# A fused attention and feed-forward kernel: the block with both heads' keys on 128 rows from pair 2 on

## The chip, the cores and the metric

The kernel runs on one core of a Trainium2 chip. The metric is the device time of one execution in microseconds. Three runs of the kernel before took 1225.55, 1228.04 and 1230.18 us; their median is 1228.04. The engines are TensorE (PE; its weight loads are shown apart as PEld), VectorE (DVE), ScalarE (ACT), GpSimd (POOL) and SyncE (SP), which issues the transfers.

## The reference

Attention for 4 batches of 12 heads over 448 positions of 64 values, and then two feed-forward layers over the 1792 rows of 768 values that it gives. All inputs and the output are float32.

```python
q_n, k_n = rmsnorm(q, g_q), rmsnorm(k, g_k)
scores = (q_n @ k_n.T) / 8                      # per batch and head, 448 x 448
attn = exp(scores - scores.max(-1)); attn = attn / (attn.sum(-1) + 1e-9)
x = heads_side_by_side(attn @ v)                # 1792 x 768
x = ((x @ w1) * (x @ w2) @ w3) @ w_out          # widths 1024, 1024, 768
h = x @ w_in                                    # width 2048
out = (h * clip(h + 3, 0, 6) / 6) @ w_out2
```

## The kernel before

**Pairs and slots.** The heads are taken in 24 pairs (`NP`), and a pair is worked through in 8 slots, one for each of two heads `j` and four blocks of 112 queries. In a slot `score` (L552) makes the scores of one block in PSUM with two matmuls (L561, L562), DVE scales them and takes their maximum (L568, L575), and ACT takes the exponential with its sum (L580). The values are then in `PP`, with queries on the rows and 2 x 448 keys, both heads side by side, on the columns.

**Blocks of keys.** The product with V needs the keys on the rows, so eight slots later `trans` (L583) turns 128 columns of `PP` at a time with four transposes (L587). The 2 x 448 = 896 columns make seven blocks, `kb` 0 to 6. Blocks 0 to 2 hold keys of the first head and 4 to 6 keys of the second. Block 3 holds both: the last 64 keys of the first head on rows 0 to 63, and 64 keys of the second on rows 64 to 127. The keys of the second head are laid out so that this comes out even.

**High and low parts.** Except in pairs 0 and 1 (`FULL`), a block is multiplied in two parts: `thi` (L593) has ACT write the high part `hi` (L596), rounded to the type fp32r, and `tlo` (L601) has DVE write the rest `lo` (L606). `vo` holds V in the same two parts side by side, 128 columns for each block, and `pv` (L611) adds the products of both parts into a bank of the head (L639 for `hi`, L640 for `lo`).

**Block 3.** For pairs 2 to 11 (`i < K3`, `K3 = 12`) block 3 is made like the others, and `pv` multiplies it with four matmuls of 64 rows each (L627): for each head `j` its own 64 rows of `hi`, and then of `lo`. From pair 12 on the parts are laid out by head: of the first head `hi` takes the high part on rows 0 to 63 (L598) and its low part on rows 64 to 127 (L608); of the second `lo` takes the high part on rows 64 to 127 (L599) and its low part on rows 0 to 63 (L609). Then one matmul of 128 rows for each head (L630) does for high and low together. The V rows of block 3 hold the same 64 keys of a head twice.

**What lies beside it.** TensorE also does the matmuls of the first feed-forward layers between those of the attention: `fill` (L384) emits some of them in every slot, by a budget (`rate`, L786), in threes (L81 to L83), first with weights that are prepared on the way (`wprime`) and then for whole batches (`layer1`, `layer2`). Their weights arrive by DMA as `raw` and are split by ACT (L137, L138, L203, L287), DVE (L140, L143) and POOL (L205, L289). The last layers follow the attention from some 630 us on.

**Order and banks.** The order on each engine comes out of a planner that simulates the program with assumed costs, `schedule_with_timeline_sim` (L982); `issue_after` pins some operations behind others. PSUM has two banks each for scores (`s`), transposes (`t`), attention products (`v`) and feed-forward products (`f`), so a transpose waits until both parts of the block before the last were written.

Of the kernel before, what the change touches and what calls it, by code (L numbers as in the profile page):

```python
# [23 lines left out]
B, H, S, D = 4, 12, 448, 64  # L24
# [15 lines left out]
FULL = (0, 1)  # L40
LG = 8
AHEAD = 3
K3 = 12
SHIFT = {'ssum': -1, 'vsplit': -2, 'load_v': 2, 'rsum1': -1, 'ksplit': 4, 'rms1': 0}


# [1 line left out]
def fused_kernel(ctx: ExitStack, tc: tile.TileContext, nat, qT, kT, vin, gq, gk,  # L48
                 w12, w3t, wo, win, wo2, outT):
    nc = tc.nc  # L50
# [34 lines left out]
    def bank(tag, name="bank"):  # L85
        return pp.tile([P, 512], F32, tag=tag, name=name)
# [317 lines left out]
    T = {}  # L404
    anchors = {}

    def attention(ap, rate):
        def full(i):
            return i in FULL
# [182 lines left out]

        def thi(i, kb):  # L593
            ps, hi, lo = T["X", i, kb]
            if kb != 3 or i < K3 or full(i):
                nc.scalar.activation(hi, ps, AF.Copy)  # L596
            else:
                nc.scalar.activation(hi[0:64, :], ps[0:64, :], AF.Copy)  # L598
                nc.scalar.activation(lo[64:128, :], ps[64:128, :], AF.Copy)  # L599

        def tlo(i, kb):  # L601
            ps, hi, lo = T["X", i, kb]
            if full(i):
                return
            if kb != 3 or i < K3:
                nc.vector.tensor_sub(lo, ps, hi)  # L606
            else:
                nc.vector.tensor_sub(hi[64:128, :], ps[0:64, :], hi[0:64, :])  # L608
                nc.vector.tensor_sub(lo[0:64, :], ps[64:128, :], lo[64:128, :])  # L609

        def pv(i, kb):  # L611
            _, hi, lo = T.pop(("X", i, kb))
            vo = T["V", i]
            if kb == 0:
                T["pv", i, 0] = bank("v")
            if kb == 3:
                T["pv", i, 1] = bank("v")
                for j in range(2):
                    if full(i):
                        z = slice(64 * j, 64 * j + 64)  # L620
                        nc.tensor.matmul(T["pv", i, j][:64, :S], vo[z, j, 3], hi[z, :], start=j == 1, stop=j == 0)
                        continue
                    if i < K3:
                        z = slice(64 * j, 64 * j + 64)
                        w = vo[z, j, 3].rearrange("p a d -> p (a d)")
                        for y in (hi, lo):
                            nc.tensor.matmul(T["pv", i, j][:, :S], w, y[z, :],  # L627
                                             start=(j == 1 and y is hi), stop=(j == 0 and y is lo))
                        continue
                    nc.tensor.matmul(T["pv", i, j][:, :S], vo[:, j, 3].rearrange("p a d -> p (a d)"),  # L630
                                     (hi, lo)[j], start=(j == 1), stop=(j == 0))
                return
            j = kb // 4
            if full(i):
                nc.tensor.matmul(T["pv", i, j][:64, :S], vo[:, j, kb % 4], hi, start=kb == 0, stop=kb == 6)
                return
            w = vo[:, j, kb % 4].rearrange("p a d -> p (a d)")
            ps = T["pv", i, j][:, :S]
            nc.tensor.matmul(ps, w, hi, start=(kb == 0), stop=False)  # L639
            nc.tensor.matmul(ps, w, lo, start=False, stop=(kb == 6))  # L640
# [116 lines left out]
        while t < 8 * NP + 23 or xs_ready:  # L757
            t += 1
            if t == 4:
                first.close()  # L760
            now[0] = t
            live = t < 8 * NP
            ps = score(*divmod(t, 8)) if live else None
            if 0 < t <= 8 * NP:
                expo(*divmod(t - 1, 8))
            u = t - LG
            if 0 <= u < 8 * NP and u % 8 < 7:
                trans(*divmod(u, 8))
            if 0 <= u - 1 < 8 * NP and (u - 1) % 8 < 7:
                tlo(*divmod(u - 1, 8))  # L770
            if live:
                scale_max(t // 8, t % 8, ps)
                negate(*divmod(t, 8))
            if 0 <= u < 8 * NP and u % 8 < 7:
                thi(*divmod(u, 8))
            if 0 <= u - 2 < 8 * NP and (u - 2) % 8 < 7:
                pv(*divmod(u - 2, 8))
            with ExitStack() as es:
                for a in anchors.get(t - (3 if "pool" in L else 2), ()):
                    es.enter_context(tc.issue_after(a.ins))  # L780
                fill(*rate(t))
            run_tasks()
            if "pool" in L:
                xnext()
# [103 lines left out]
    for b, t in enumerate(order):  # L888
        acc = None
        for m in range(M2):  # L890
# [14 lines left out]
            w = wnext  # L905
# [80 lines left out]
```

## Time and profile before

| | |
|---|---|
| median of three runs | 1228.04 us (1225.55 to 1230.18) |
| profiled execution | 1225.79 us, its span 1224.0 us |
| TensorE busy | 1162.5 us (95%) |
| weight loads | 1023.3 us (84%) |
| DVE, ACT, POOL busy | 754.0, 727.5 and 465.5 us |
| read from and written to memory | 173.93 and 28.68 MB |

The span runs from the first to the last instruction of the profiled execution; the time of that execution also counts what lies around it. Busy times overlap between engines. A matmul's duration counts its way through the array, so that successive matmuls overlap; the distance of their starts is what one of them takes of TensorE's time.

### The profile page before, as it was taken

How to read it: one execution, taken by the hardware profiler on the slowest of the kernel's cores; microseconds unless marked ns; L12 is line 12 of the kernel's file. 1: busy time of each engine (PE TensorE's matmuls, PEld its weight loads, DVE VectorE, ACT ScalarE, POOL GpSimd, SP SyncE). 2: the span in 40 equal slices, each digit the busy share in tenths (PEclk: the TensorE clock that was granted, in tenths of full speed). 3: DMA queues.
4: the chain of work that ended last, by engine and by line, in shares of the span. 5: the costliest groups of instructions: out<-in, count | busy, mean ns of one | idle time of the engine just before them, and what ended most of it. 6: DMA issues, size and time to landing. Idle time of an engine off the chain costs nothing.

```text
span 1224.0 us, 16942 instructions
## 1 busy us (share of the span) xinstructions
PE 1162.5 (95%) x5868; PEld 1023.3 (84%) x5868; DVE 754.0 (62%) x1474; ACT 727.5 (59%) x1401; POOL 465.5 (38%) x316
## 2 busy tenths in 40 slices
PE   3698998999899999999999999999999999999998
PEld 2457887777789999889999998999999999999997
DVE  7977988989757787667624446884433433343332
ACT  6888788888767767766534336664433443344332
POOL 3534234544432213221020005555444554554452
PEclk9698998999999999999999999999999999999999
DMA  8677656788887677666359895430200020001001
GB/s 273 213 218 238 187 188 203 249 287 284 281 296 253 209 243 236 231 213 211 137 194 407 323 328 199 155 100 23 91 1 1 1 91 1 1 1 46 1 1 46
DMA packets 64694, 203.73 MB, mean 166 GB/s; under 512 B 8544, under 2 KB 25440, under 8 KB 64608
## 3 DMA queue, kind: packets, MB, share of 16 engines
q1 hardware_dynamic: 64608, 202.65, 49.4%
q8 instruction: 46, 0.75, 0.2%
q14 instruction: 40, 0.33, 0.1%
HBM read 173.93 MB, written 28.68 MB: 166 GB/s over the span
## 4 chain that ended last, share of the span: by engine, by line
PE 68%; ACT 3%; DMA 2%; DVE 1%; issue 1%; POOL 1%; SPq 0%; POOLq 0%; ACTq 0%; DVEq 0%
PE bank L81 7%; PE bank L83 7%; PE bank L82 7%; PE acc L83 6%; PE acc L82 6%; PE acc L81 6%; PE h L81 6%; PE h L82 6%; PE h L83 6%; PE bank L587 2%; PE bank L561 1%; PE bank L562 1%; PE bank L639 1%; PE bank L640 1%; DMA rsb<-rsd 1%; ACT PP L580 1%
## 5 line engine op out<-in xcount | busy, mean ns | idle before, releaser
L847 POOL TENSOR_TENSOR wis<-wf,wis 128x768 fp32r<-128x768 f32 x63 | 120.4, 1911 | 228.1 <-ACT wis L846 228.1
L926 DVE SCALAR_TENSOR_TENSOR u<-u,h 128x448 f32<-128x448 f32 x64 | 39.6, 619 | 210.6 <-ACT u L925 210.6
L847 POOL TENSOR_TENSOR wos<-wf,wos 128x768 fp32r<-128x768 f32 x64 | 120.5, 1883 | 90.4 <-ACT wos L846 89.1
L580 ACT ACTIVATE PP<-PP,mx 112x448 f32<-112x448 f32 x192 | 127.7, 667 | 39.4 <-DVE mx L575 35.0
L568 DVE CUSTOM_DVE_ANT_0 PP<-bank,rb,rq 112x448 f32<-112x448 f32 x192 | 129.2, 676 | 30.7 <-PE bank L562 24.0
L83 PE MATMUL bank<-xhl,ws 128*128 128x448 f32 x384 | 142.1, 370 | 4.6 <-POOL ws L289 4.6
L81 PE MATMUL bank<-xhl,ws 128*128 128x448 f32 x384 | 143.8, 374 | 0.8 <-ACT ws L287 0.8
L82 PE MATMUL bank<-xhl,ws 128*128 128x448 f32 x384 | 141.6, 369 | 0.0
L82 PE MATMUL acc<-g,wos 128*128 128x448 f32 x384 | 141.3, 368 | 0.0
L83 PE MATMUL acc<-g,wos 128*128 128x448 f32 x384 | 141.3, 368 | 0.0
L81 PE MATMUL acc<-g,wos 128*128 128x448 f32 x384 | 139.3, 368 | 0.0
L81 PE MATMUL h<-x2h,wis 128*128 128x448 f32 x378 | 139.0, 368 | 0.0
L83 PE MATMUL h<-x2h,wis 128*128 128x448 f32 x378 | 137.5, 364 | 1.6 <-POOL wis L847 1.6
L82 PE MATMUL h<-x2h,wis 128*128 128x448 f32 x378 | 138.9, 367 | 0.0
L925 ACT ACTIVATE u<-h,half 128x448 f32<-128x448 f32 x64 | 40.8, 637 | 158.0 <-PE h L83 158.0
L930 DVE TENSOR_TENSOR g<-u,g 128x448 fp32r<-128x448 f32 x64 | 103.9, 1623 | 37.4 <-ACT g L929 37.4
L606 DVE TENSOR_TENSOR xl<-bank,xh 128x448 fp32r<-128x448 f32 x142 | 87.3, 617 | 30.7 <-ACT xh L596 29.2
L846 ACT ACTIVATE wos<-wf 128x768 fp32r<-128x768 f32 x64 | 54.2, 847 | 86.0 <-PE acc L83 85.7
L596 ACT ACTIVATE xh<-bank 128x448 fp32r<-128x448 f32 (+1 forms) x156 | 83.3, 541 | 33.0 <-PE bank L587 31.7
L587 PEld LDWEIGHTS bank<-ident,PP 112*128 112x128 f32 x672 | 78.6, 142 | 26.4 <-issue 8.6
L587 PE MATMUL bank<-ident,PP 112*128 112x112 f32 x672 | 95.1, 264 | 5.5 <-DVE xl L606 4.7
L561 PE MATMUL bank<-K,Q 128*112 128x448 f32 x192 | 77.4, 404 | 23.8 <-DVE mx L568 12.7
(136 smaller groups left out, 2754.1 us busy)
## 6 DMA issues: line engine op xcount, KB each, us to landing
ws<-w12d SPq DMA_DIRECT2D x48, 768.0 KB
ws<-wpd SPq DMA_DIRECT2D x32, 768.0 KB
raw<-in_w_dram SPq DMA_DIRECT2D x32, 384.0 KB
w12d<-ws SPq DMA_DIRECT2D x16, 768.0 KB
wr<-in_wo_dram SPq DMA_DIRECT2D x16, 768.0 KB
qr<-in_qT_dram SPq DMA_DIRECT2D x24, 448.0 KB
kr<-in_kT_dram SPq DMA_DIRECT2D x24, 448.0 KB
nat<-in_nat_dram SPq DMA_DIRECT2D x23, 448.0 KB
```

The source lines that it names most:

```text
L81: nc.tensor.matmul(ps, lh, rh, start=first, stop=False)
L82: nc.tensor.matmul(ps, lh, rl, start=False, stop=False)
L83: return nc.tensor.matmul(ps, ll, rh, start=False, stop=last)
L561: nc.tensor.matmul(ps[:CP, :S], qs, k1[:, j, :], start=True, stop=False)
L568: anchors[8 * i + s].append(nc.vector.tensor_tensor_reduce(out=T["PP", i][:, c, sl], in0=ps[:CP, :S], in1=T["rb", i][:, sl], op0=ALU.mult, ...
L580: anchors[8 * i + s].append(nc.scalar.activation(v, v, AF.Exp, bias=T["m", i][:, 8 + s : 9 + s], accum_out=T["sum", i][:, s : s + 1]))
L587: nc.tensor.transpose(ps[:, c * CP : c * CP + CP], src[:, c, kb * P : kb * P + P], ident[:CP, :CP])
L596: nc.scalar.activation(hi, ps, AF.Copy)
L606: nc.vector.tensor_sub(lo, ps, hi)
L846: nc.scalar.activation(t[:, 0, :], wf[q], AF.Copy)
L847: nc.gpsimd.tensor_sub(t[:, 1, :], wf[q], t[:, 0, :])
L930: nc.vector.tensor_sub(g[:, 1, :], u, g[:, 0, :])]
```

## The change

The constant `K3` goes. In `thi`, `tlo` and `pv` the layout by head for block 3 holds for all pairs but 0 and 1, that is from pair 2 on. The four matmuls of 64 rows are removed from the code.

```diff
-K3 = 12
 ...
         def thi(i, kb):
             ps, hi, lo = T["X", i, kb]
-            if kb != 3 or i < K3 or full(i):
+            if kb != 3 or full(i):
                 nc.scalar.activation(hi, ps, AF.Copy)
             else:
                 nc.scalar.activation(hi[0:64, :], ps[0:64, :], AF.Copy)
 ...
-            if kb != 3 or i < K3:
+            if kb != 3:
                 nc.vector.tensor_sub(lo, ps, hi)
             else:
                 nc.vector.tensor_sub(hi[64:128, :], ps[0:64, :], hi[0:64, :])
 ...
-                    if i < K3:
-                        z = slice(64 * j, 64 * j + 64)
-                        w = vo[z, j, 3].rearrange("p a d -> p (a d)")
-                        for y in (hi, lo):
-                            nc.tensor.matmul(T["pv", i, j][:, :S], w, y[z, :],
-                                             start=(j == 1 and y is hi), stop=(j == 0 and y is lo))
-                        continue
                     nc.tensor.matmul(T["pv", i, j][:, :S], vo[:, j, 3].rearrange("p a d -> p (a d)"),
                                      (hi, lo)[j], start=(j == 1), stop=(j == 0))
```

## Rows read from the trace of the kernel before

**Rows 1.** The page: busy us of each engine, share of the span, instructions.
```profile
PE 1162.5 (95%) x5868; PEld 1023.3 (84%) x5868; DVE 754.0 (62%) x1474; ACT 727.5 (59%) x1401; POOL 465.5 (38%) x316
```

**Rows 2.** Windows: stretch, its us, busy us by engine (instructions), clock, DMA, GB/s.
```profile
112.00:142.00 30.00, 30.00 (x175) 27.18 (x175) 21.09 (x48) 19.15 (x42) 12.08 (x10) 1.00 0.74 235
142.00:322.00 180.00, 160.34 (x825) 132.27 (x824) 160.40 (x396) 152.27 (x341) 83.75 (x69) 0.95 0.72 235
322.00:352.00 30.00, 30.00 (x159) 25.46 (x158) 22.71 (x58) 21.22 (x47) 12.68 (x11) 1.00 0.94 321
352.00:640.00 288.00, 286.11 (x1587) 258.79 (x1586) 198.81 (x519) 186.46 (x401) 64.27 (x55) 1.00 0.66 216
```

**Rows 3.** Chain of waits, 324 to 352 us: shares by engine, tile and line.
```profile
by line: PE bank L81 20.5%; PE bank L83 19.7%; PE bank L82 18.8%; PE bank L587 12.1%; PE bank L627 7.1%; PE bank L561 6.4%; PE bank L562 5.8%; PE bank L639 5.1%; PE bank L640 4.6%; PE bank L495 0.4%
```

**Rows 4.** TensorE's waits, 142 to 322 us: us in total, times, longest.
```profile
PE bank L83 <- POOL ws L289: 4.6, 4, 2.7
PE bank L561 <- DVE mx L568: 3.2, 8, 0.5
PE bank L587 <- DVE xl L606: 3.0, 4, 1.4
```

**Rows 5.** By line: ns least/median/most, first and last start; who waited for L599.
```profile
L599 ACT ACTIVATE xl<-bank x12: 539/540/543, 368.9 to 618.5; 64x448 fp32r<-64x448 f32 x12
  DVE xh L608: 6.2, 8
...
L606 DVE TENSOR_TENSOR xl<-bank,xh x142: 570/618/627, 100.9 to 626.3; 128x448 fp32r<-128x448 f32 x142
...
L609 DVE TENSOR_TENSOR xl<-bank,xl x12: 625/626/627, 370.1 to 619.8; 64x448 fp32r<-64x448 f32 x12
```

**Rows 6.** Timeline of TensorE, a block of pair 4: start us, us, instruction.
```profile
161.95 0.34 PE L82 MATMUL bank<-woh,w 128*128 128x384 f32 x1
162.13 0.34 PE L83 MATMUL bank<-woh,w 128*128 128x384 f32 x1
162.40 0.47 PE L627 MATMUL bank<-xh,vo 64*128 64x448 f32 x2
162.80 0.60 PE L587 MATMUL bank<-ident,PP 112*128 112x112 f32 x4
163.33 0.47 PE L627 MATMUL bank<-xl,vo 64*128 64x448 f32 x2
163.73 0.44 PE L81 MATMUL bank<-woh,w 128*128 128x384 f32 x1
164.01 0.34 PE L82 MATMUL bank<-woh,w 128*128 128x384 f32 x1
```

**Rows 7.** Windows of L627 alone: stretch, TensorE busy, weight loads, clock, DMA, GB/s.
```profile
112.00:142.00 30.00, 1.88 (x6) 0.74 (x6) 1.00 0.74 235
142.00:322.00 180.00, 6.68 (x26) 2.65 (x26) 0.95 0.72 235
322.00:352.00 30.00, 2.34 (x8) 0.92 (x8) 1.00 0.94 321
```

**Rows 8.** Timeline of TensorE, a block of pair 12.
```profile
372.88 0.37 PE L630 MATMUL bank<-xh,vo 128*128 128x448 f32 x1
373.09 0.37 PE L81 MATMUL bank<-abh,ws 128*128 128x448 f32 x1
...
373.50 0.55 PE L587 MATMUL bank<-ident,PP 112*128 112x112 f32 x4
373.82 0.45 PE L630 MATMUL bank<-xl,vo 128*128 128x448 f32 x1
374.11 0.55 PE L587 MATMUL bank<-ident,PP 112*128 112x112 f32 x4
```

**Rows 9.** A wait of TensorE (timeline), and the window behind it.
```profile
185.19 0.44 PE L83 MATMUL bank<-woh,w 128*128 128x384 f32 x1 [2.02 <-POOL w L205]
...
185.50:188.90 3.40, 3.40 (x15) 2.42 (x13) 1.77 (x5) 3.40 (x10) 3.22 (x3) 0.54 0.72 221
```

## Prediction

> **What bounds the kernel now.** I read the page first. TensorE is busy for 95% of the span, DVE for 62% and ACT for 59% [rows 1]. So TensorE work taken out is worth its time wherever TensorE never rests, and what is added to DVE and ACT costs time where it makes TensorE rest. The change touches pairs 2 to 11, whose last-block products lie between 119 and 347 us, so I asked for that stretch cut into windows [rows 2]. From 112 to 142 and from 322 to 352 TensorE is busy for every microsecond, with DVE at 70% and 76% and ACT at 64% and 71%. From 142 to 322 TensorE rests for 180 - 160.34 = 19.7 us, DVE is busy for 160.40 (89%) and ACT for 152.27 (85%): three engines that take turns as the one that is late, and the granted clock is 0.95 and not 1.00. From 352 to 640 us TensorE is busy for 286.11 of 288. The chain of waits confirms the second edge: in 324 to 352 us it is TensorE alone, and L627 is 7.1% of it, 2.0 us [rows 3]. The three largest of TensorE's waits in the middle stretch are for POOL's weight halves, 4.6 us, and twice for DVE, 3.2 + 3.0 = 6.2 us [rows 4].
>
> **What TensorE loses: the 64-row visits.** One pair's last block has four matmuls on 64 rows (L627) and gets two on 128 rows (L630). Their durations alone, 4 x 0.47 against 0.37 + 0.45 [rows 6, 8], would give 1.06 us a pair, but matmuls overlap, so I go by starts. In the timeline the two L627 matmuls of a visit stand as one piece, "x2", of 0.47 us: they run side by side on the two halves of the rows [rows 6]. So the four cost two visits, not four turns. A visit still costs more than a turn of a full matmul. From 162.13 to 164.01 are 1.88 us, in which lie L83, two visits with four transposes (L587) between them, and L81. Ordinary starts there are 0.18 apart (161.95 to 162.13); less twice that, the two visits with the transposes take 1.52. In the layout by head, 372.88 to 374.11 are 1.23 us, less 0.41 for the two other matmuls inside (373.09 to 373.50): 0.82 for two L630 and four transposes [rows 8]. One L630 is 0.21 (372.88 to 373.09), so the transposes are 0.40, and a visit is (1.52 - 0.40) / 2 = 0.56. Of it 0.40 pass from its start to the next one; the rest is at its edges, 0.27 us from the L83 before it and 0.28 from the L81 behind it to the next, where 0.18 is usual [rows 6].
>
> The windows for L627 give the visits [rows 7]: 6 matmuls in 1.88 us busy are 4 visits of 0.47 in the first full stretch (one pair's high parts came apart into two), 8 in 2.34 are 5 in the second (the same), and 26 in the middle are 13. 22 visits by 0.56 are 12.3 us. What comes instead is 20 full matmuls by 0.21, 4.2 us. By stretch: first -(4 x 0.56 - 3 x 0.21) = -1.6; second -(5 x 0.56 - 4 x 0.21) = -2.0; middle -(13 x 0.56 - 13 x 0.21) = -4.5. TensorE sheds 8.1 us in all. The bounds are -10.6 (1.06 a pair by bare durations) and -0.4 (a visit at the 0.21 of a turn, so that only the two that came apart are saved).
>
> A rule of the Trainium skill speaks against this change: "TensorE: Matmul & The Clock Gate", Part 3 (Packing small matmuls), The mechanism, has matmuls in different row groups run together in about the time of one, some 4 ns apart, so that four on half the rows would cost what two on all of them cost. This trace agrees that two run as one piece of 0.47 us; it does not agree that the visit is as cheap as a turn, since 0.40 us pass to the next start and not 0.18 to 0.21 [rows 6]. "TensorEngine Tiling (Array Packing)", Tiling Modes, Key Properties, says that changing the mode drains the engine, which would account for the edges.
>
> **What ACT and DVE get.** An operation on 64 rows takes as long as one on 128: L609 on 64 takes 0.626 us, L606 on 128 takes 0.618 [rows 5]. So two for one adds a whole one: 0.54 us of ACT a pair, by L599, and 0.63 of DVE, by L609. From pair 12 on DVE also sat idle for L599 before L608, 6.2 us in 8 of 12 pairs [rows 5], 0.5 us a pair. Neither addition touches a DMA, SP's or POOL's queue. In the full stretches there are 7 and 9 us of DVE left in 30, and 11 and 9 of ACT; 3.5 pairs add some 2.2 and 1.9 us, so they are covered, as pairs 12 to 23 are, where TensorE rested for 1.9 us in 288 [rows 2]. If that cover were gone it would cost 3.5 x 0.63 = 2.2 us.
>
> In the middle 6.5 pairs add 4.1 us to DVE and 3.5 to ACT, in front of operations on which TensorE already waits. Behind L608 and L609 are queued DVE's next score maximum (L568), which frees the score bank, and the next block's L606, which frees the transpose bank; TensorE waits for exactly these [rows 4]. Bounds: at best nothing shows, since ACT and DVE have 28 and 20 us of rest in these 180; at worst each pair's serial chain is longer by 0.54 + 0.63 + 0.5 = 1.67, +10.9 us. I take DVE's 4.1 in full and nothing of ACT's: DVE is as busy as TensorE there, and its two waits together are more than POOL's. The middle then gives -4.5 + 4.1 = -0.4.
>
> **Sum.** -1.6 - 2.0 - 0.4 = -4.0 us. The profiled execution took 1225.79 us (span 1224.0 and 1.8 around it); it would become 1221.8. It lies 2.25 below the median of the runs shown, so against the median it is 1228.04 - 4.0 = 1224.0.
>
> **Rivals.** *All of it arrives.* If DVE's and ACT's operations fit into their 20 and 28 us of rest, the whole 8.1 counts: 1228.0 - 8.1 = 1219.9. For it: TensorE bounds what follows and pairs 12 to 23 run this way without loss. Against: the middle stretch, where TensorE's waits on DVE of 6.2 us show that DVE's rest is not where TensorE needs it.
>
> *The middle is a loop through ACT and DVE: slower.* Transposes, high part, low part, product, with two banks for the transposes. Where this loop and not TensorE sets the pace, the TensorE time saved becomes waiting, and the loop grows by 0.54 + 0.63 in each of 6.5 pairs: +7.6 us. Waits also cost clock: after TensorE had rested 2.02 us before 185.19, the granted clock of 185.5 to 188.9 was 0.54, nearly the lower of its two levels (1.2 of 2.4 GHz) [rows 9]; 3.4 us at 0.54 lose 1.6. Two more such dips are 3.2. With -3.6 from the full stretches: 7.6 + 3.2 - 3.6 = +7.2, 1235. It decides from the point where half of the 6.5 blocks are waited for by TensorE. For it: DVE at 89% and ACT at 85% leave TensorE little that they can do late. Against: the longest wait there, 2.7 us, is for POOL, which gets nothing more to do.
>
> *The visits were free.* If two matmuls side by side take one turn of 0.21 and the time around them belongs to something else, TensorE sheds only 0.4, and DVE's 4.1 in the middle remain: 1228.0 + 3.7 = 1231.7. For it: the two do run as one piece. Against: the starts of rows 6. The first page named above gives this rule in the Trainium skill.
>
> *Another order.* The order on every engine is a planner's, made from assumed costs. Ten pairs of changed operations change the plan from 119 us on, and a wait such as the 2.02 us with the dip of 1.6 behind it [rows 9] may come or go: some 4 us to either side of my sum, 1220 or 1228. Nothing in the trace gives it a sign.
>
> **How the numbers follow.** Chances: my sum 0.38 (its own range 1221 to 1227), all of it 0.24, the slower loop 0.22, free visits 0.07, another order 0.09. About 0.5%, 6.1 us, is what a measurement of this kernel can tell from no change, so faster means under 1221.9 and slower over 1234.2. Faster: 0.20 of the second, 0.06 of my own and 0.03 of the order make 0.29. Slower: 0.16 of the loop and 0.03 of the two others make 0.19. The rest, 0.52, is no change. The range is 1216 to 1236: below, all savings with a wait of 4 us gone besides; above, the loop with its dips and 1 us more.
>
> **What would show it.** Right: no L627; L630 20 times more, with its neighbours 0.21 apart; L598, L599, L608 and L609 22 times each; TensorE still at 100% on either side of the middle; waits on L606, L608 and L609 up by about 4 us in the middle; the stretch after 352 us as long as before. Wrong: waits on DVE and ACT unchanged (then 1220), waits up by over 10 us with more half-clock stretches (1235), or a shift that stands behind POOL or a DMA, which would be the order and not these operations.

## The result, and the profile after

The change made the kernel slower: 1233.57 us against 1226.45, medians of 20 runs each; the ratio is 1.0056 with a 95% interval of 1.0044 to 1.0068, so 6.9 us with 5.4 to 8.3. The forecast of 1224 had the wrong sign, 4.0 us less than a median of three runs that lay 1.6 us above that of the 20; the time lies in the range, near its slow end. The profiled execution of the kernel after took 1229.62 us, 3.8 more than the one of before, so it shows only part of the loss. In the kernel after, the lines of the attention stand one lower, the matmul on 128 rows is L622, the products of the other blocks are L631 and L632.

What the change says, it did. By source line (columns as in [rows 5]) the products on 128 rows are there 22 times for each head, 10 more than the 12 of [rows 5], and so is DVE's first low part (L607), which the first product reads:

```profile
L622 PE MATMUL bank<-xh,vo x22: 363/368/475, 119.1 to 626.8; 128*128 128x448 f32 x22
L622 PE MATMUL bank<-xl,vo x22: 444/450/722, 119.6 to 628.2; 128*128 128x448 f32 x22
...
L607 DVE TENSOR_TENSOR xh<-bank,xh x22: 617/618/619, 113.4 to 622.9; 64x448 fp32r<-64x448 f32 x22
```

The windows answer to [rows 2]:

```profile
112.00:142.00 30.00, 29.30 (x175) 27.35 (x173) 22.87 (x52) 21.01 (x45) 14.07 (x11) 1.00 0.74 231
142.00:322.00 180.00, 155.48 (x791) 129.82 (x792) 167.52 (x395) 150.91 (x333) 78.62 (x67) 0.94 0.71 227
322.00:352.00 30.00, 27.72 (x143) 22.35 (x143) 23.89 (x62) 26.01 (x60) 13.21 (x13) 1.00 0.97 335
352.00:640.00 288.00, 287.47 (x1593) 259.39 (x1592) 199.31 (x525) 188.18 (x405) 65.86 (x55) 1.00 0.67 219
```

TensorE's rest in the middle grew from 19.7 to 24.5 us, and the two stretches in which it never rested have rests of 0.7 and 2.3. DVE is busier in the middle by 7.1 us and TensorE gets 34 matmuls fewer done there (791 for 825). From 352 to 640 us TensorE is as busy as before (287.5 and 286.1 of 288). TensorE's waits from 142 to 322 us answer to [rows 4]:

```profile
PE bank L622 <- DVE xh L607: 8.2, 4, 3.0
PE bank L560 <- DVE mx L567: 4.8, 5, 1.3
PE bank L80 <- ACT ws L286: 3.2, 2, 2.1
PE bank L631 <- ACT xh L595: 2.8, 3, 2.0
PE bank L586 <- DVE xl L605: 2.2, 3, 1.2
PE bank L586 <- DVE xl L608: 1.1, 4, 0.3
...
PE bank L82 <- POOL ws L288: 0.3, 1, 0.3
```

The waits on POOL's weight halves, the largest before, are nearly gone, and a new one leads: the first product on 128 rows waits for DVE, 8.2 us in four places. Before, the high products needed ACT's high part alone; now the first product needs DVE too. The longest of the four, in the timeline of the kernel after (pair 5; lines left out between):

```profile
187.62 0.52 ACT L597 ACTIVATE xh<-bank 64x448 fp32r<-64x448 f32 x1
...
188.10 1.08 DVE L476 TENSOR_TENSOR rt<-ry 112x32 f32<-112x32 f32 x1
188.15 0.54 ACT L598 ACTIVATE xl<-bank 64x448 fp32r<-64x448 f32 x1
...
189.22 0.94 DVE L478 TENSOR_TENSOR rt<-rt,ss 112x32 f32<-112x32 f32 x1
...
190.74 0.90 DVE L483 TENSOR_TENSOR rr<-ry,rt 112x32 f32<-112x32 f32 x1
...
191.67 0.62 DVE L607 TENSOR_TENSOR xh<-bank,xh 64x448 fp32r<-64x448 f32 x1
...
192.32 0.63 DVE L608 TENSOR_TENSOR xl<-bank,xl 64x448 fp32r<-64x448 f32 x1
...
192.34 0.47 PE L622 MATMUL bank<-xh,vo 128*128 128x448 f32 x1 [2.98 <-DVE xh L607]
```

ACT was done at 188.69. DVE came to the block 3 us later, behind other work of its queue. The windows of the kernel after before and behind this wait (columns as in [rows 2]):

```profile
188.80:192.20 3.40, 0.56 (x4) 0.24 (x2) 3.30 (x6) 3.38 (x9) 2.33 (x3) 1.00 0.93 265
194.10:197.50 3.40, 3.01 (x11) 2.45 (x10) 3.19 (x9) 0.69 (x2) 0.00 (x0) 0.51 0.50 202
```

TensorE was busy for 0.56 of 3.4 us, and then the granted clock was 0.51, the lower level, as in [rows 9].

All this could be the cause, or an effect of another order: on TensorE the planner's order differs in many places from 119 us on.

### The profile page after: what moved, and what is told of

Same layout as the page of the kernel before. It is cut to its first block, busy times and chain, and to the rows that moved or that the text cites. A ratio compares the mean times of both kernels' runs of the same rounds, so it can differ in the third digit from the quotient of the medians.

```text
span 1227.8 us, 16926 instructions
## 1 busy us (share of the span) xinstructions
PE 1159.6 (94%) x5848; PEld 1022.4 (83%) x5848; DVE 764.7 (62%) x1484; ACT 734.5 (60%) x1411; POOL 464.2 (38%) x316
## 4 chain that ended last, share of the span: by engine, by line
PE 75%; DMA 7%; ACT 6%; issue 5%; DVE 4%; POOL 3%; SPq 0%; POOLq 0%; ACTq 0%; DVEq 0%
PE bank L80 9%; PE bank L81 9%; PE bank L82 8%; PE acc L80 6%; PE acc L81 6%; PE acc L82 6%; PE h L80 6%; PE h L81 6%; PE h L82 6%; PE bank L586 4%; DMA raw<-in_w_dram 2%; PE bank L560 2%; PE bank L561 2%; PE bank L631 2%; PE bank L632 2%
## 5 line engine op out<-in xcount | busy, mean ns | idle before, releaser
L918 DVE SCALAR_TENSOR_TENSOR u<-u,h 128x448 f32<-128x448 f32 x64 | 39.7, 620 | 210.5 <-ACT u L917 210.5
L80 PE MATMUL h<-x2h,wis 128*128 128x448 f32 x378 | 139.0, 368 | 0.0
L605 DVE TENSOR_TENSOR xl<-bank,xh 128x448 fp32r<-128x448 f32 x132 | 81.2, 616 | 27.2 <-ACT xh L595 25.6
L595 ACT ACTIVATE xh<-bank 128x448 fp32r<-128x448 f32 (+1 forms) x146 | 77.7, 539 | 27.0 <-PE bank L586 24.8
```

The costliest lines, as they stand in the source:

```text
L80: nc.tensor.matmul(ps, lh, rh, start=first, stop=False)
```

## The experiments

Each was timed in five rounds beside the kernel before on the same chip; 1% is 12.3 us. In what follows the loss of 6.9 us is taken apart.

**First round: the planner free.** *low_first* changes only the order of the four products on 64 rows.

```diff
-                        for y in (hi, lo):
+                        for y in (lo, hi):
...
-                                             start=(j == 1 and y is hi), stop=(j == 0 and y is lo))
+                                             start=(j == 1 and y is lo), stop=(j == 0 and y is hi))
```

> The kernel before, with the four 64-row products of block 3 in pairs 2 to 11 in another order: low parts first, then high parts. No work is added; TensorE's first visit then needs DVE's low part, not ACT's high part alone. Theory of the product's wait (the layout by head makes TensorE wait for DVE's queue, 8.2 us at four places in the trace after): slower than before by 5 us or more, 1232 or above, with waits of the first visit on DVE. Theory of DVE's time (0.63 us a pair more on DVE): no change, 1225 to 1228. Theory of the plan (another order of the engines, whatever the edit): anything within 4 us, no such waits.

0.9961 (0.9946 to 0.9977): 4.8 us faster. The forecast of the product's wait missed, but the wait itself was not tested: the trace has no wait of L627 on DVE. The same work in another order moved the time by most of what was to be explained. So an edit with a free planner can't be read as the cost of its operations.

*pe_only* gives TensorE its two products and leaves ACT and DVE as they were (in `pv` alone `if i < K3` becomes `if False`).

> ACT and DVE work as in the kernel before, one operation each for block 3, and TensorE takes the two 128-row products in pairs 2 to 11 all the same: of the high part for the first head, of the low part for the second, so the block's product leaves out half of its terms and mixes heads. TensorE's saving alone. The product's wait: the first product needs ACT alone, so the 8.1 us worked out for TensorE arrive, 1217 to 1221. DVE's time: the same, 1217 to 1221. The plan: 1222 to 1231, no gain that can be told from the order.

1.0007 (0.9986 to 1.0027). TensorE's saving did not arrive, or the order hid it.

*ops_only* adds the work of ACT and DVE alone.

```diff
+            if kb == 3 and i < K3 and not full(i):
+                for z in (slice(0, 64), slice(64, 128)):
+                    nc.scalar.activation(hi[z, :], ps[z, :], AF.Copy)
...
+            if kb == 3 and i < K3:
+                for z in (slice(0, 64), slice(64, 128)):
+                    nc.vector.tensor_sub(lo[z, :], ps[z, :], hi[z, :])
```

> The kernel before, with block 3 in pairs 2 to 11 written by two ACT and two DVE operations of 64 rows each, every half in its own place, and the four 64-row products as before. Only the added work. The product's wait: high products still need ACT alone, so little: 0 to 3 us more, 1226 to 1229.5. DVE's time: 4 to 7 us more, 1230.5 to 1233.5. The plan: anything within 4 us.

1.0046 (1.0029 to 1.0063), 5.6 us: about the loss, without any product on 128 rows.

*late* emits the products of block 3 of the kernel after at the start of the next slot.

> The kernel after, with the two products of block 3 in pairs 2 to 11 emitted at the start of the next slot, behind that slot's feed-forward matmuls, so that DVE has about 2 us more until TensorE comes to them. The product's wait: the waits of L630 on L608 fall from 8.2 to under 2.5 us and most of the loss goes, 1220 to 1227. DVE's time: no change from after, 1232 to 1235. The plan: anything within 4 us of after.

1.0045 (1.0027 to 1.0063), no help. But the test missed its aim: in the trace the first product stands behind the same six feed-forward matmuls as in the kernel after, and the waits of L630 on L608 were still 7.4 us. It tells nothing of the wait.

**Second round: the order held.** The planner's order of the kernel before, instruction by instruction and for every engine, was written into the program as edges from each instruction to the one before it on its engine. An added operation stands right behind the one it was split from, the first product of 128 rows in the place of the high visit, the second in that of the low visit. In the traces TensorE, ACT, DVE and POOL then work through the instructions of before in the same order, so that kernels differ by their operations alone. In the edit, `at` holds one engine's instructions in the order of before.

```diff
+        for y, z in zip(at, at[1:]):
+            tc.add_manual_dep(z[2], y[2].name, mybir.DependencyInfo(mybir.DependencyClass.NoSync, mybir.DependencyReason.DATA), reason='hold')
```

> The kernel before, unchanged, with the order of the instructions of every engine written into it as edges (the order that the planner had found for it). A control: all theories expect the time of before, within 2 us.

1.0001 (0.9984 to 1.0018): holding the order costs nothing that can be told (-2.0 to 2.2 us).

> The whole change, with the order of before held on every engine: the second ACT and the second DVE operation of a block stand right behind the first, the first 128-row product stands where the high visit stood, the second where the low visit stood. Nothing but the operations differs from before. The product's wait: the first product now stands too early for DVE, slower than before by 4 us or more, 1231 to 1240. DVE's time: TensorE's 8 us against some 4 us, 1221 to 1226. The plan (the loss comes from the other order alone): the loss is gone and TensorE's saving shows, 1218 to 1225.

1.0037 (1.0018 to 1.0055), 4.5 us (2.2 to 6.8). The loss is mostly the operations', and the plan's theory fell; what the free order of the kernel after adds, 0.19%, lies within the two intervals.

> The order of before held; block 3 in pairs 2 to 11 is written by two ACT and two DVE operations of 64 rows, each half in its own place, and the 64-row products stay. The product's wait: 0 to 3 us more than before, 1226 to 1230. DVE's time: 3 to 6 us more, 1230 to 1234. The plan: within 2 us of before, since the 5.6 us that this edit cost with a free order came from the order.

1.0046 (1.0024 to 1.0068), 5.6 us (2.9 to 8.4), the same as with a free order.

> The order of before held; ACT and DVE as before, and the two 128-row products in pairs 2 to 11, so that the product of block 3 leaves out half of its terms and mixes heads. TensorE's saving with nothing else moved. The product's wait and DVE's time: 6 to 8 us less, 1218 to 1222. The plan: the same 6 to 8 us, which a free order had hidden. No gain here would mean that TensorE's time in this stretch is not worth anything.

0.9993 (0.9979 to 1.0006), 0.9 us less. So of the 8.1 us that TensorE was to save about one arrives, against the 6 to 8 that all three theories had. The two parts add up: 5.6 - 0.9 = 4.7 for 4.5 measured. The product's wait is in the trace of held_change, where the first product waits for DVE for 6.2 us in five places (112 to 352 us). But held_ops has no such product and costs as much, so no loss of its own can be told for this wait.

As the order is the same, the profiled executions can be laid on each other. Starts of the first score matmul of some pairs, in us:

| pair | before | held | held_pe | held_dve | held_act | held_ops | held_change | spare_act (fourth round) |
|---|---|---|---|---|---|---|---|---|
| 5 | 138.0 | 137.8 | 138.1 | 136.5 | 137.1 | 137.3 | 137.8 | 137.9 |
| 7 | 180.1 | 180.0 | 180.4 | 179.1 | 181.0 | 180.9 | 181.6 | 181.3 |
| 8 | 207.3 | 206.3 | 207.6 | 207.6 | 209.5 | 210.5 | 211.3 | 209.7 |
| 9 | 226.5 | 226.0 | 226.1 | 227.9 | 228.9 | 233.2 | 234.1 | 229.5 |
| 13 | 350.8 | 350.5 | 350.9 | 354.6 | 355.5 | 358.7 | 358.7 | 353.0 |

held_ops and held_change fall behind held by some 8 us between pair 5 and pair 9, where the last blocks of pairs 3 to 6 are worked on; held_act and held_dve by 3 to 4 there and by 2 more up to pair 13. held_pe runs level with before throughout. The table can't be read to a few us, since one execution of each kernel is shown: held ends 3.4 us after before (spans 1227.4 and 1224.0 us), though it starts pair 13 earlier, and held_ops, 8.2 us behind held at pair 13, ends 3.2 behind it. What the place is worth is told by the times of held_3to6 and held_rest below.

**Third round: which operation, and where.** In *held_dve* only the subtraction is in two, in *held_act* only the copy of the high part.

> The order of before held; of the added work of pairs 2 to 11 only DVE's: the low part is written by two operations of 64 rows, the high part by one of ACT, the four products stay. Theory of the loop (in 140 to 217 us, pairs 3 to 6, TensorE, ACT and DVE hand the block round one after the other, and each added operation costs its own length there): half of the 5.6 us, 4 x 0.63 = 2.5 us, 1229 to 1232. Theory of DVE alone (ACT has room, DVE is the one that is late): all of the 5.6, 1232 to 1234.5. Theory of ACT alone: nothing, 1226.5 to 1228.5.

1.0018 (1.0003 to 1.0033), 2.2 us (0.4 to 4.0), as the loop says.

> The order of before held; of the added work of pairs 2 to 11 only ACT's: the high part is written by two operations of 64 rows, the low part by one of DVE, the four products stay. The loop: 4 x 0.54 = 2.2 us more, 1229 to 1231.5. DVE alone: nothing, 1226.5 to 1228.5. ACT alone: all of the 5.6, 1232 to 1234.5.

1.0043 (1.0028 to 1.0059), 5.3 us (3.4 to 7.2), for ACT's operation, which the prediction had for nothing. The loop, with 2.2 us, missed here; the theory of ACT alone has this run right and DVE's wrong. ACT's operation seems to cost more than DVE's, though the two intervals overlap, and 5.3 + 2.2 is more than the 5.6 of both together, within the noise. How a cost arises can be seen in the timeline of TensorE at pair 4. First the kernel held, then held_act: the next block's product, and the windows around it.

```profile
164.31 0.48 PE L723 MATMUL bank<-xh,vo 128*128 128x448 f32 x1
...
163.80:167.10 3.30, 2.48 (x11) 1.28 (x11) 2.97 (x7) 2.92 (x7) 2.20 (x2) 1.00 0.64 187
167.20:170.50 3.30, 3.30 (x21) 3.14 (x20) 3.24 (x9) 0.54 (x1) 0.00 (x0) 1.00 0.97 327
```

```profile
164.47 0.47 PE L728 MATMUL bank<-xh,vo 128*128 128x448 f32 x1 [0.95 <-ACT xh L683]
...
163.80:167.10 3.30, 1.96 (x9) 1.25 (x10) 3.00 (x7) 3.04 (x7) 2.18 (x2) 1.00 0.73 219
167.20:170.50 3.30, 3.30 (x14) 3.11 (x12) 3.24 (x9) 0.00 (x0) 0.00 (x0) 0.50 0.94 270
```

ACT comes to the next block's high part later, TensorE waits 0.95 us where no wait was, and the 3.3 us behind are granted at 0.50 and not 1.00: 14 matmuls for 21. From the feed-forward matmul before this wait to the score matmul behind the dip held takes 5.6 us (163.84 to 169.47) and held_act 7.8 (163.18 to 171.00): an operation of 0.54 us has cost over two. The dip is not always paid for. Between 142 and 323 us the kernel before has five stretches of 3.4 us at the lower level, held three and held_pe seven, and their times are the same within the noise.

How much of the loss is clock can be estimated from the mean granted clock that every run lists. One minus it, times the span, is what TensorE would lose if it were busy at the lower level throughout. Against the kernel before in the same rounds this estimate grows by 2.0 us in held_act (clock 0.9808 for 0.9824), by 3.4 in held_ops (0.9793 for 0.9820) and by 4.4 in held_3to6 below (0.9789 for 0.9824), and not in held_dve (0.9828 for 0.9824); each is uncertain by 2 to 3 us. So between a third and nearly all of the loss may be lost clock behind such waits. No run separates the two.

*held_3to6* and *held_rest* make the whole change in some pairs only.

> The order of before held; the whole change, but only in pairs 3 to 6 (and from 12 on, as before). The loop: the loss of the whole change lies here, 4 to 6 us, 1231.5 to 1234. Rival, a cost spread over all ten pairs: 4 tenths of the 4.6 us of the whole change, 1.8 us, 1228.5 to 1230.

1.0037 (1.0020 to 1.0054), 4.5 us: as much as the change in all ten pairs.

> The order of before held; the whole change in pairs 2 and 7 to 11 (and from 12 on, as before), not in 3 to 6. The loop: no loss and some of TensorE's saving, 0 to 3 us less than before, 1224.5 to 1228. Rival, a cost spread over all ten pairs: 6 tenths of 4.6 us, 2.8 us more, 1229.5 to 1231.5.

0.9988 (0.9971 to 1.0005), 1.5 us less (-3.6 to 0.6), not told from nothing. The cost is not spread; it lies in pairs 3 to 6.

**Fourth round: two questions left.** *spare_act* has an operation of ACT of the same length in the same place, for which nobody waits.

```diff
                 nc.scalar.activation(hi, ps, AF.Copy)
+                if kb == 3 and not full(i):
+                    more(i, nc.scalar.activation(spare[0:64, :], spare[0:64, :], AF.Copy))
```

> The order of before held, the kernel before otherwise; behind the high part of block 3 in pairs 2 to 11 ACT does one more copy of 64 x 448 inside a spare tile that nobody reads. It takes ACT's time in the same place as the second operation of the change, but no product and no subtraction waits for it. If ACT's queue is the bound there: 4 to 6 us more, as with the real second operation, 1231.5 to 1234. If the cost is the block's own way from ACT to DVE to TensorE: under 1.5 us, 1227 to 1229.5.

1.0009 (0.9996 to 1.0022), 1.1 us (-0.5 to 2.7). Its group in spare_act (name, shapes, count; busy, mean ns, idle before) shows that it took the time; below it stand the next block's product at pair 4 and a window behind it, as shown for held_act:

```profile
L685 ACT ACTIVATE spare<-spare 64x448 bf16<-64x448 bf16 x10 | 5.7, 571 | 0.0
...
164.67 0.47 PE L728 MATMUL bank<-xh,vo 128*128 128x448 f32 x1 [0.57 <-ACT xh L683]
...
167.60:171.00 3.40, 3.40 (x14) 3.20 (x13) 3.34 (x9) 0.00 (x0) 0.00 (x0) 0.50 0.99 321
```

By the times, the same 0.57 us in the same place costs less when the block does not wait for it (up to 2.7 us, against 3.4 or more), as the account by the block's own way from TensorE over ACT and DVE back to TensorE had it. The traces don't bear this account out. At pair 4 spare_act has the wait and the dip of held_act, made by ACT's queue alone, and it starts pair 9 at 229.5 us, 3.5 behind held and no earlier than held_act (228.9). The two part only later, at pair 13 with 353.0 and 355.5 us; from 232 to 322 us the granted clock is 0.98 in spare_act and 0.94 in held_act. Over all runs spare_act's clock is not below that of before (0.9831 for 0.9818). So whether the block's way, ACT's queue or the clock behind the waits makes the real operation dear stays open.

> The order of before held; the whole change only in pairs 2, 10 and 11 (and from 12 on), whose last blocks lie where TensorE was busy all the time. If TensorE is the bound there: 2 to 4 us less, 1224 to 1226. If its saving is worth nothing there either: within 1 us of before, 1227 to 1229.

1.0006 (0.9991 to 1.0021). No gain where TensorE had been busy without rest. Laid on the kernel held, by the starts of the same feed-forward matmuls, held_edges gains 0.7 us at pair 2 (from -1.2 at 115.5 us to -1.9 at 120.7) and 1.1 at pair 11 (from +0.9 at 341.3 to -0.2 at 346.2). At pair 2, held first, then held_edges:

```profile
115.48 0.34 PE L162 MATMUL bank<-woh,w 128*128 128x384 f32 x1
...
120.74 0.34 PE L161 MATMUL bank<-woh,w 128*128 128x384 f32 x1
```

```profile
114.33 0.34 PE L163 MATMUL bank<-woh,w 128*128 128x384 f32 x1
...
118.82 0.34 PE L162 MATMUL bank<-woh,w 128*128 128x384 f32 x1
```

This gain has gone by 139.0 us (-0.5). At pair 10 one sees how a gain can go. ACT in the kernel held, and then ACT and TensorE in held_edges:

```profile
324.62 0.56 ACT L217 ACTIVATE raw<-raw 128x384 f32<-128x384 f32 x1 [3.07 <-DMA raw<-in_w_dram]
...
325.51 0.53 ACT L680 ACTIVATE xh<-bank 128x448 fp32r<-128x448 f32 x1
```

```profile
325.95 0.56 ACT L218 ACTIVATE raw<-raw 128x384 f32<-128x384 f32 x1 [3.28 <-DMA raw<-in_w_dram]
...
326.85 0.52 ACT L681 ACTIVATE xh<-bank 128x448 fp32r<-128x448 f32 x1
...
327.51 0.62 DVE L691 TENSOR_TENSOR xl<-bank,xh 128x448 fp32r<-128x448 f32 x1
...
328.18 0.47 PE L727 MATMUL bank<-xl,vo 128*128 128x448 f32 x1 [0.29 <-DVE xl L691]
```

The weight transfer on which ACT waits came 1.3 us later here, the next block's high part stands behind it in ACT's queue, and TensorE, which had been early, waits. Whether the transfer was late by chance or by the change, one execution does not tell.

## Why the prediction was wrong

**TensorE's term was sized right and worth little.** The step "TensorE sheds 8.1 us in all" holds in place where it was looked at: pair 2 gained 0.7 us, for 2 x 0.56 - 2 x 0.21 = 0.7 by the prediction's prices, and pair 11 gained 1.1 for 3 x 0.56 - 2 x 0.21 = 1.26. That a visit is two matmuls side by side and yet dearer than a turn was right. What failed is the step from there to the end: the full stretches were to give -1.6 and -2.0, of which -2.7 in pairs 2, 10 and 11, and held_edges shows +0.7 us there (-1.1 to +2.6). "Busy for every microsecond" was read as "TensorE sets the pace". It shows only that no gap was left. At pair 10, the one place followed up, the block after the saving waits for ACT and DVE, and ACT for a weight transfer; that the other gains went the same way is not shown. The measured worth of the whole saving is 0.9 us (-0.7 to 2.6).

**ACT's term was missing.** "I take DVE's 4.1 in full and nothing of ACT's" failed too: ACT's operation alone cost 5.3 us, DVE's 2.2, both together 5.6. The reasons for the choice were DVE's busy share, 89% for ACT's 85% [rows 2], and its waits; neither told that ACT's operation was free.

**The slower rival came nearest, and its time in part by luck.** It gave 1235, 7.2 us more, with a chance of 0.22: ACT's and DVE's lengths added in a loop, TensorE's saving turned into waiting, half-clock stretches behind the waits. Added work of both engines and a saving that does not arrive are what the runs show. But its errors cancel: its place was too wide (7.6 us for 6.5 pairs; the loss lies in pairs 3 to 6, where the same lengths give 4 x (0.54 + 0.63) = 4.7), and so was its discount (3.6 us, of which held_edges shows nothing). The lengths also miss ACT's run alone, 4 x 0.54 = 2.2 us for 5.3. Its argument against itself, that the longest wait was for POOL, did not save the kernel: with the order held, TensorE's waits on POOL (112 to 352 us) are 3.4 us in held and 4.3 in held_change, and the loss comes all the same; with a free order they went from 6.6 us before (4.6 in [rows 4] and 2.0 in [rows 9]) to 0.3.

**The others.** "Another order" is real, low_first moved 4.8 us by it, but the change's loss stays with the order held. "The visits were free" does not fit the gains in place. That pairs 12 to 23 carry the layout without loss was no argument for the earlier pairs: DVE and ACT are busy there for 69% and 65% of 352 to 640 us [rows 2].

## What to carry to other kernels

An engine that is busy for all of a stretch need not set its pace where a planner fills its gaps: before a saving is counted, look at what the saved engine waits for next, and whether that came any earlier. In a loop over several engines price every added operation, also that of the engine with more rest, and expect more where a wait takes the clock down. Here the lengths in four pairs add up to 4.7 us and the runs gave 4.5 to 5.6, but the split between the two engines did not follow the lengths. Where a planner orders the work, hold the order before comparing operations; a free order moved the same work by 0.4%.

## What the runs showed of the hardware

Half the rows save nothing on ACT and DVE: in the kernel after, at 188 to 193 us, ACT took 0.54 us on 64 rows (L598) and on 128 (L595), DVE 0.63 (L608) and 0.62 (L605). On TensorE two matmuls of 64 rows run together, but cost 0.56 us among full matmuls for 0.21 of one full matmul (the prediction's estimates from [rows 6, 8], which the gains at pairs 2 and 11 fit).

DVE's small operations on operands in SBUF have two durations. By source line, in the kernel after:

```profile
L476 DVE TENSOR_TENSOR rt<-ry x12: 175/186/1083, 11.4 to 543.9; 112x32 f32<-112x32 f32 x12
```

Of its twelve, eight took 0.18 us on average, with POOL at rest for at least half of their time; four beside a POOL operation took 1.06. L476 is one of three such operations, of 0.90 to 1.08 us, among those that stood in front of L607 above. The Trainium skill, "SBUF — State Buffer", "SBUF: two separate sides", says that a VectorE operation with two SBUF inputs and a GpSimd operation that reads SBUF lock one shared pair of ports against each other, and that the later of them is blocked for the whole of the other's instruction. This trace agrees: 0.18 and 1.06 us for one operation.
